# A fused strided-attention, MoE and FFN kernel: all strided heads in compact classes, another order of the first loads, up sums in place, three score buffers, a higher fill rate

## The chip, the cores and the metric

The kernel runs on one core of a Trainium2 chip. The metric is device time in microseconds of one execution. The core has a matmul engine (TensorE, PE in the profile), three engines for elementwise work (VectorE is DVE, ScalarE is ACT, GpSimd is POOL), SyncE (SP), which only issues DMA transfers here, and 16 DMA engines.

## The reference, cut to what matters

```python
# attention: q, k, v of 4 batches, 8 heads, 576 positions, 64 dimensions
scores = scale * np.matmul(q, k.transpose(0, 1, 3, 2))
rel = pos[:, None] - pos[None, :]
mask_local = (rel >= 0) & (rel < 32)
mask_strided = (rel >= 0) & (pos[None, :] % 32 == pos[:, None] % 32)
# heads 0..3 use mask_local, heads 4..7 mask_strided; softmax; times v
# MoE: 2304 tokens, 512 wide, 8 experts of 1024; gate weights balanced in 8 rounds
h = np.maximum(x @ w1[e], 0.0); out += P[:, e:e+1] * (h @ w2[e])
# FFN: 512 -> 2048 -> 512
h = x @ w_in; g = h / (1 + np.exp(-1.702 * h)); return g @ w_out
```

A strided head needs little of its 576 x 576 scores: position p sees only positions with the same remainder by 32, so the head falls into 32 classes of 18 positions each.

## The kernel before, in words

**Attention.** Heads are handled in pairs, pairs 0 and 1 local, 2 and 3 strided. The list `groups` (line 866 on) says in which order; an entry is (batch, pair, g). For g of 0 to 2 a group is *wide*: `att_scores` multiplies queries and keys of two pieces for two heads (for a strided pair a piece is seven classes of 18, 126 rows, and the third group has one piece of 72), VectorE masks and takes the maximum, ScalarE takes the exponential, GpSimd divides, `att_transpose` transposes on TensorE, `att_values` multiplies by the values. With g = -1 a group is *compact* and stands for a whole strided pair: `compact_scores` runs 64 small matmuls of 18 columns that place the classes side by side (each shows as two records in the trace), VectorE transposes 32 x 32 blocks, ScalarE copies the result into a zeroed wide tile (`ew`), and `compact_values` multiplies four classes at a time, 72 columns. Before the change batches 0 and 1 have their strided pairs compact, batches 2 and 3 wide, three groups each.

**Steps.** `att_step(i)` runs five stages for five neighbouring groups, so that a group's scores come at its step i, its values at i + 4. Between the stages `fill` puts other work on TensorE: idle matmuls for the first ten steps, a few half products and idle matmuls for the next six, and then *pieces*, RATE of them per fill, three fills a step. Queries and keys are loaded by `LOAD_QK`, values by `LOAD_V`, at the ends of steps worked out from `groups`.

**Pieces.** The MoE and the FFN are cut in units of 256 hidden columns for a block of 768 tokens. A unit is one round of a seven-product scheme: `PRODUCTS` lists seven products of an input (or a sum of inputs) with a weight quarter W or a sum of quarters T. Every operand is split in a high and a low part, and a product is six matmuls (`sum_of_six`, line 1017). A unit has 13 pieces: seven products (pieces 0, 2, ... 12 of the unit) and, between them, six times six matmuls with the down weights of the unit before (`tile_down`, lines 1282 to 1284). `side[g]` holds what is handed to the other engines after piece g.

**Weights.** For each of the 32 MoE units, the up weights are loaded (`load_w1`), GpSimd forms the four sums T1 to T4 (`sums_w1`, lines 235 to 237) in a tile of its own, and `split_w1` splits quarters and sums: ScalarE copies the high part (lines 258, 268), VectorE or GpSimd subtracts (line 252), and the result goes to the products and by DMA to a store in device memory for later blocks. `plan_weights` says at which piece each is handed out. The down weights get the same treatment (`plan_down_sums`, line 343).

**The start.** The loads stand in order: queries and keys of the first two pairs, one compact value, the first up weights, a second compact value, the first down weights, two compact values of batch 1, the gate weights, the second up weights; then come the attention's steps. Masks and constants go by ScalarE's queue. All on SP's queue is issued in order; a transfer into a buffer that is still read waits there.

Of the kernel before, what the change touches and what calls it, by code (L numbers as in the profile page):

```python
# [15 lines left out]
P = 128  # L16
# [20 lines left out]
RATE = 1.15  # L37
# [20 lines left out]
def strided_attention_moe_ffn(  # L58
# [26 lines left out]
    CPT = P // CLEN  # L85
# [142 lines left out]
    def sums_w1(i, t=None):  # L228

        r = raw[1, i]  # L230
        if t is None:
            t = rawp[0].tile([P, 4, 2 * P], F32, tag="sums", name="sums")
        g = nc.gpsimd
# [7 lines left out]
    WHERE = {"W11": (1, 0), "W12": (1, 1), "W21": (1, 2), "W22": (1, 3), "T1": (3, 0), "T3": (3, 1), "T2": (3, 2), "T4": (3, 3)}  # L241

    def quarter(i, what):
        which, q = WHERE[what]
        return raw[which, i][:, q, :]
# [84 lines left out]
    def plan_down_sums(dp, i, again=None):  # L330
# [59 lines left out]
    def plan_weights():  # L390

        for at, k in zip((10, 12, 14, 16, 18, 19, 21), range(NPR)):
            side[at].append(lambda k=k: split_w1(PLAIN, k))
        side[8].append(lambda: [t() for t in sums_w1(PLAIN)])
        for i in range(PLAIN - 1, NU):
            new = [fresh(u) for u in range(i, i + 3)]

            if PLAIN <= i < NU - 1:
                if new[1]:
                    side[piece_at(i, 0)].append(lambda i=i: [t() for t in sums_w1(i + 1)])  # L400
                for m, k in enumerate((0, 3, 5, 1, 2, 4, 6) if new[1] else range(NPR)):
                    at = max(m, 2 * (m - 2) + 1)
                    side[piece_at(i, at)].append(lambda i=i, k=k: split_w1(i + 1, k))
# [223 lines left out]
    wide_of = {}  # L627

    def open_wide(m):
        t = xcp.tile([P, 2 * CQ, CG * CLEN], F32, tag="xc", name="ew")  # L630
        nc.gpsimd.memset(t, 0.0)
        wide_of[m] = t
# [6 lines left out]
    def compact_scores(i, b, pair):  # L639
# [14 lines left out]
        e = ap.tile([P, 4 * P], F32, tag="e", name="e", bufs=4)  # L654
# [5 lines left out]
        def mask():  # L660
            for j in range(2):
# [4 lines left out]
                    in1=msk[:, None, 5 * P : 5 * P + CLEN].to_broadcast([P, CQ, CLEN]),  # L666
# [26 lines left out]
    def compact_transpose(i, b, pair):  # L693
# [3 lines left out]
        w = att[b, pair, -1] = wide_of[pair % 2]  # L697
        src = eT.rearrange("p n (m q) -> p (n m) q", q=Q)
        for c in range(CG):
            rows = slice(c * Q, c * Q + CLEN)  # L700
            nc.scalar.activation(out=w[rows, :, c * CLEN : (c + 1) * CLEN], in_=src[rows, :, :CLEN], func=AF.Copy)

    def compact_values(i, b, pair):
        w = att.pop((b, pair, -1))
# [3 lines left out]
        for h in range(2):  # L708
            if i < NALONE:
                av = ps.tile([P, 512], F32, tag="AB"[h], name="av")  # L710
            elif h:
                av = ps.tile([P, 512], F32, tag="B", name="av")
            else:
                av = eps.tile([P, 512], F32, tag="pa", name="av")
            for m in range(CQ // 2):
                g = h * CQ // 2 + m
                for j in range(2):
# [3 lines left out]
                        rhs=w[:, j * CQ + g, :],  # L721
# [14 lines left out]
    def geometry(pair, g, u):  # L736

        if pair < NPAIR // 2:
            q0 = (2 * g + u) * QT
            return q0, QT, max(0, q0 - STRIDE), P  # L740
        t = 2 * g + u
        c0 = t * CPT
        n = min(CPT, NCLS - c0) * CLEN
        return c0 * CLEN, n, c0 * CLEN, n

    def units(pair, g):
        return 2 if pair < NPAIR // 2 or g < 2 else 1

    def att_scores(i, b, pair, g):
        qkt = att_in["qk", b, pair]  # L750
        U = units(pair, g)

        sc = eps.tile([P, 2, 512], F32, tag="sc", name="sc")
        for u in range(U):
            for j in range(2):
                q0, R, k0, C = geometry(pair, g, u)
# [8 lines left out]
        e = ap.tile([P, 4 * P], F32, tag="e", name="e", bufs=4)  # L765
        st = ap.tile([P, 2, 4], F32, tag="st", name="st", bufs=4)
        m0 = 3 * P if pair >= NPAIR // 2 else P if g else 0
# [79 lines left out]
    def att_keep(b, pair, g, av, U, R):  # L847
        n = U * R
        if pair < NPAIR // 2:
            blk, at = divmod(b * S + g * 2 * QT, BT)  # L850
            nc.vector.tensor_copy(xblk[blk][:, pair, at : at + n], av[:, :n])
            return
        strided_keep(b, pair, 2 * g * CPT, n // CLEN, av)

# [16 lines left out]
    groups += [(b, pair, g) for b in range(2, B) for pair in PAIRS for g in range(3)]  # L871
# [13 lines left out]
    wide = [p for p in pairs if groups[at[p][0]][2] >= 0]  # L885
# [3 lines left out]
    for n, p in enumerate(wide):  # L889
        LOAD_V[max(at[wide[n - 2]][-1] + 4 if n > 1 else 0, at[p][0] + 1)].append(p)  # L890
# [530 lines left out]
    with tc.manual_schedule():  # L1421
# [209 lines left out]
```

## Time and profile before

| | before |
|---|---|
| runs, median (lowest to highest) | 1957.82 us (1957.12 to 1961.69) of 3 |
| profiled execution | 1956.79 us, its span 1955.0 us |
| TensorE busy, share of the span | 1919.4 us, 98% |
| VectorE, ScalarE, GpSimd busy | 1455.9, 864.3, 1242.0 us |
| mean granted TensorE clock | 0.994 of full |

The span is the part of the execution between the first and the last instruction. "Busy" is the time in which an engine has an instruction running. A row of the groups gives line, engine, operation, tiles, shapes and count, then busy time and mean time of one, then the idle time before it with what ended it. "<-DMA qkt<-qk" says that a wait ended when the transfer into `qkt` landed; "<-issue" that no semaphore or transfer that the profile knows ended it. Times of a timeline are us from the start of the span.

### The profile page before, as it was taken

How to read it: one execution, taken by the hardware profiler on the slowest of the kernel's cores; microseconds unless marked ns; L12 is line 12 of the kernel's file. 1: busy time of each engine (PE TensorE's matmuls, PEld its weight loads, DVE VectorE, ACT ScalarE, POOL GpSimd, SP SyncE). 2: the span in 40 equal slices, each digit the busy share in tenths (PEclk: the TensorE clock that was granted, in tenths of full speed). 3: DMA queues.
4: the chain of work that ended last, by engine and by line, in shares of the span. 5: the costliest groups of instructions: out<-in, count | busy, mean ns of one | idle time of the engine just before them, and what ended most of it. 6: DMA issues, size and time to landing. Idle time of an engine off the chain costs nothing.

```text
span 1955.0 us, 34399 instructions
## 1 busy us (share of the span) xinstructions
PE 1919.4 (98%) x11276; PEld 1793.0 (92%) x11276; DVE 1455.9 (74%) x2751; ACT 864.3 (44%) x2152; POOL 1242.0 (64%) x1249
## 2 busy tenths in 40 slices
PE   6999999999999999999999999999999999999999
PEld 5777888898888999999999999999999998888888
DVE  4787778777766788788878788888886766756555
ACT  4555556676665333333333433333333445533332
POOL 3456666777777677677777888888887767600100
PEclk8999999999999999999999999999999999999999
DMA  5457779999997898888898888999988867665653
GB/s 213 152 209 270 266 276 331 385 338 350 379 330 248 318 307 290 297 286 283 285 303 286 253 310 293 341 327 322 364 314 314 294 222 265 237 189 187 222 192 121
DMA packets 283649, 545.75 MB, mean 279 GB/s; under 512 B 30832, under 2 KB 51536, under 8 KB 282576
## 3 DMA queue, kind: packets, MB, share of 16 engines
q1 hardware_dynamic: 283184, 543.09, 80.5%
q8 instruction: 91, 1.49, 0.3%
q14 instruction: 86, 0.70, 0.1%
q10 hardware_dynamic: 288, 0.47, 0.1%
HBM read 381.90 MB, written 161.53 MB: 278 GB/s over the span
## 4 chain that ended last, share of the span: by engine, by line
PE 80%; DVE 2%; POOL 1%; ACT 0%; issue 0%; DMA 0%; ACTq 0%; DVEq 0%
PE y L1177 22%; PE pA L1017 22%; PE pC L1017 11%; PE y L1284 6%; PE y L1283 6%; PE y L1282 6%; PE pB L1017 5%; DVE xs L552 0%; POOL s L1149 0%; POOL comb L1124 0%; DVE comb L1124 0%; POOL xc L568 0%; DVE xc L572 0%; DVE r L1130 0%; DMA w<-s1moe 0%
## 5 line engine op out<-in xcount | busy, mean ns | idle before, releaser
L1017 PE MATMUL pA<-xc,w 128*128 128x384 f32 x2880 | 572.3, 336 | 1.9 <-DVE pB L1072 1.9
L1177 PE MATMUL y<-comb,w 128*128 128x384 f32 x2688 | 537.6, 334 | 1.4 <-DVE sum L1187 1.4
L1017 PEld LDWEIGHTS pA<-xc,w 128*128 128x128 f32 x2880 | 508.0, 188 | 18.8 <-DVE pB L1072 2.9
L1177 PEld LDWEIGHTS y<-comb,w 128*128 128x128 f32 x2688 | 472.0, 188 | 2.5 <-DVE sum L1187 2.4
L1124 POOL TENSOR_TENSOR comb<-s,comb 128x384 fp32r<-128x384 f32 x256 | 283.3, 1117 | 89.1 <-ACT comb L1119 82.4
L1187 DVE TENSOR_TENSOR sum<-y,sum 128x384 f32<-128x384 f32 x420 | 231.4, 552 | 98.5 <-PE y L1177 96.8
L1017 PE MATMUL pC<-xc,w 128*128 128x384 f32 x1464 | 295.0, 336 | 0.0
L1017 PEld LDWEIGHTS pC<-xc,w 128*128 128x128 f32 x1464 | 258.6, 188 | 10.0
L1284 PE MATMUL y<-w,hl 128*128 128x512 f32 x672 | 266.9, 397 | 0.4 <-DVE hl L1056 0.4
L1282 PE MATMUL y<-w,hh 128*128 128x512 f32 x672 | 263.4, 392 | 3.7 <-DVE acc L1297 2.0
L1283 PE MATMUL y<-w,hh 128*128 128x512 f32 x672 | 265.3, 395 | 0.0
L1119 ACT ACTIVATE comb<-r 128x384 fp32r<-128x384 f32 x192 | 101.0, 526 | 364.0 <-DVE r L1130 348.3
L252 POOL TENSOR_TENSOR w<-raw,w 128x512 fp32r<-128x512 f32 (+1 forms) x100 | 117.6, 1182 | 74.4 <-ACT w L258 69.9
L1284 PEld LDWEIGHTS y<-w,hl 128*128 128x128 f32 x672 | 125.9, 187 | 28.3 <-DVE hl L1056 1.0
L1282 PEld LDWEIGHTS y<-w,hh 128*128 128x128 f32 x672 | 126.2, 188 | 22.8 <-DVE acc L1297 2.6
L1017 PE MATMUL pB<-xc,w 128*128 128x384 f32 x708 | 142.4, 335 | 0.0
L1283 PEld LDWEIGHTS y<-w,hh 128*128 128x128 f32 x672 | 126.0, 187 | 15.9
L1124 POOL TENSOR_TENSOR comb<-r,comb 128x384 fp32r<-128x384 f32 x64 | 67.5, 1054 | 114.4 <-ACT comb L1119 114.4
L1119 ACT ACTIVATE comb<-s 128x384 fp32r<-128x384 f32 x256 | 131.5, 514 | 11.0 <-POOL s L1149 10.9
L1149 POOL TENSOR_TENSOR s<-r,r 128x384 f32<-128x384 f32 x127 | 134.8, 1082 | 2.1 <-DVE r L1130 2.0
L1311 DVE TENSOR_TENSOR acc<-y,acc 128x512 f32<-128x512 f32 x126 | 86.8, 689 | 63.3 <-PE y L1284 63.1
L1017 PEld LDWEIGHTS pB<-xc,w 128*128 128x128 f32 x708 | 125.2, 188 | 4.7
(178 smaller groups left out, 2878.0 us busy)
## 6 DMA issues: line engine op xcount, KB each, us to landing
w<-s1moe SPq DMA_DIRECT2D x448, 256.0 KB, 4.9
w<-s7moe SPq DMA_DIRECT2D x448, 256.0 KB, 4.9
s1moe<-w SPq DMA_DIRECT2D x216, 256.0 KB, 4.5
w<-s1ffn SPq DMA_DIRECT2D x133, 256.0 KB, 2.7
s7moe<-kw SPq DMA_DIRECT2D x116, 256.0 KB, 4.9
s7moe<-w SPq DMA_DIRECT2D x96, 256.0 KB, 4.7
w<-s2ffn SPq DMA_DIRECT2D x38, 512.0 KB, 3.7
raw<-wa SPq DMA_DIRECT2D x32, 512.0 KB, 5.9
```

The lines of the kernel that those rows point to most:

```text
L252: eng.tensor_tensor(out=t[:, 1], in0=src, in1=f(high), op=ALU.subtract)
L1017: nc.tensor.matmul(out=o, lhsT=w[:, hw, kk * P : (kk + 1) * P], rhs=x[:, hx, kk, :], start=opens and m == 0, stop=ends and m == len(todo) - 1,
L1119: nc.scalar.activation(out=t[:, 0, :], in_=part[i, q], func=AF.Copy)
L1124: eng.tensor_tensor(out=t[:, 1, :], in0=part[i, q], in1=f(t[:, 0, :]), op=ALU.subtract)
L1149: eng.tensor_tensor(out=part[i, q], in0=part[i, a], in1=part[i, b], op=op)
L1177: nc.tensor.matmul(out=o, lhsT=t[:, hw, dt * P : (dt + 1) * P], rhs=x[:, hx, :], start=(n == 0), stop=(n == 5))
L1187: nc.vector.tensor_tensor(out=a, in0=o, in1=a, op=ALU.add)
L1282: nc.tensor.matmul(out=o, lhsT=hh[:, c], rhs=w[:, 0], start=(m == 0), stop=False)
L1283: nc.tensor.matmul(out=o, lhsT=hh[:, c], rhs=w[:, 1], start=False, stop=False)
L1284: nc.tensor.matmul(out=o, lhsT=hl[:, c], rhs=w[:, 0], start=False, stop=(m == 1))
L1311: nc.vector.tensor_tensor(out=a, in0=y, in1=a, op=ALU.add)
```

## The change

All strided pairs become compact: batches 2 and 3 now have four compact groups in place of twelve wide ones, so the list of groups shrinks from 40 to 32 and the steps from 44 to 36. `RATE` goes from 1.15 to 1.5. One zeroed tile `wide` takes the place of two; the score tiles `e` have three buffers in place of four; the values' buffer is eight pieces long in place of six. The first loads are put in another order: queries and keys, then two compact values, and the weights and the values of batch 1 after the first attention steps. For MoE units `sums_w1` writes T1 to T4 over the quarters they no longer need, after the quarters' own splits, with another order and other pieces in `plan_weights` and `plan_down_sums`.

```diff
-RATE = 1.15
+RATE = 1.5
@@ sums_w1
+        if t is None and UNITS[i][1] == "moe":
+            steps = [(0, 1, 0), (1, 3, 1), (3, 3, 0), (2, 2, 3)]
+            todo = [
+                lambda o=o, a=a, b=b: g.tensor_tensor(
+                    out=r[:, o, :], in0=r[:, a, :], in1=r[:, b, :], op=ALU.subtract
+                )
+                for o, a, b in steps
+            ]
+            return todo + [lambda: placed.add(i)]
@@ plan_down_sums
-            at = piece_at(i, ((3, 3, 4, 5), (0, 1, 1, 2))[i == S0 - 1][m]) if again is None else piece_at(again, 5 + m)
+            at = piece_at(i, ((1, 1, 2, 2), (0, 1, 1, 2))[i == S0 - 1][m]) if again is None else piece_at(again, 5 + m)
@@ plan_weights
-        for at, k in zip((10, 12, 14, 16, 18, 19, 21), range(NPR)):
+        for at, k in zip((10, 12, 14, 16, 18, 19, 21), (0, 3, 5, 1, 2, 4, 6)):
-        side[8].append(lambda: [t() for t in sums_w1(PLAIN)])
+        side[15].append(lambda: [t() for t in sums_w1(PLAIN)])
+                moe = UNITS[i + 1][1] == "moe"
-                    side[piece_at(i, 0)].append(lambda i=i: [t() for t in sums_w1(i + 1)])
+                    side[piece_at(i, 4 if moe else 0)].append(lambda i=i: [t() for t in sums_w1(i + 1)])
-                    at = max(m, 2 * (m - 2) + 1)
+                    at = (0, 1, 2, 5, 7, 8, 9)[m] if new[1] and moe else max(m, 2 * (m - 2) + 1)
@@ load_v
-        t = ap.tile([P, 6, P], F32, tag="v", name="vt")
-        nc.sync.dma_start(out=t, in_=vw[b, pair])
+        t = ap.tile([P, CQ, P], F32, tag="v", name="vt")
+        compact = pair >= NPAIR // 2
+        src = vc[b, pair - NPAIR // 2] if compact else vw[b, pair]
+        nc.sync.dma_start(out=t if compact else t[:, : vw.shape[3]], in_=src)
+    wide = ap.tile([P, 2 * CQ, CG * CLEN], F32, name="wide", bufs=1)
@@ compact_scores, att_scores
-        e = ap.tile([P, 4 * P], F32, tag="e", name="e", bufs=4)
+        e = ap.tile([P, 4 * P], F32, tag="e", name="e", bufs=3)
@@ compact_transpose (compact_values reads wide too)
-        w = att[b, pair, -1] = wide_of[pair % 2]
-            nc.scalar.activation(out=w[rows, :, c * CLEN : (c + 1) * CLEN], in_=src[rows, :, :CLEN], func=AF.Copy)
+            nc.scalar.activation(out=wide[rows, :, c * CLEN : (c + 1) * CLEN], in_=src[rows, :, :CLEN], func=AF.Copy)
@@ groups
-    groups += [(b, pair, g) for b in range(2, B) for pair in PAIRS for g in range(3)]
+    for b in range(2, B):
+        groups += [(b, pair, -1) for pair in PAIRS[:2]]
+        groups += [(b, pair, g) for pair in PAIRS[2:] for g in range(3)]
@@ loads
-    wide = [p for p in pairs if groups[at[p][0]][2] >= 0]
+    ring = [p for p in pairs if p[0] > 1 or p[1] < NPAIR // 2]
-    for n, p in enumerate(wide):
-        LOAD_V[max(at[wide[n - 2]][-1] + 4 if n > 1 else 0, at[p][0] + 1)].append(p)
+    for n, p in enumerate(ring):
+        LOAD_V[max(at[ring[n - 2]][-1] + 4, at[p][0] + 1) if n > 1 else n + 2].append(p)
@@ the start
-        load_vc(0, PAIRS[0])
         nc.scalar.dma_start(out=cst, in_=consts)
-        load_w1(0)
-        load_vc(0, PAIRS[1])
-        load_w2(0)
-        for m in range(2):
-            open_wide(m)
         for pair in PAIRS[:2]:
-            load_vc(1, pair)
+            load_vc(0, pair)
+        nc.gpsimd.memset(wide, 0.0)
@@ ahead: what is handed out after a step
-        load_w1(1)
+        ahead[1].append(lambda: load_w1(0))
+        ahead[3].append(lambda: load_w2(0))
+        ahead[4].append(lambda: load_w1(1))
+        for m, pair in enumerate(PAIRS[:2]):
+            ahead[5 + m].append(lambda pair=pair: load_vc(1, pair))
         for n, what in enumerate(QUARTERS):
-            ahead[3 + 2 * n].append(lambda what=what: split_plain(0, what))
+            ahead[(4, 5, 7, 8)[n]].append(lambda what=what: split_plain(0, what))
```

## Rows read from the trace of the kernel before

**Rows 1.** The page's busy line: us, share of the span, instructions.

```profile
PE 1919.4 (98%) x11276; PEld 1793.0 (92%) x11276; DVE 1455.9 (74%) x2751; ACT 864.3 (44%) x2152; POOL 1242.0 (64%) x1249
```

**Rows 2.** Busy time by stage: columns PE, PEld, DVE, ACT, POOL; clock, DMA, GB/s.

```profile
10.00:20.00 10.00, 2.60 (x52) 2.08 (x52) 2.22 (x7) 1.24 (x3) 0.67 (x1) 0.60 1.00 380
...
95.00:237.00 142.00, 137.55 (x932) 111.72 (x930) 110.79 (x251) 83.43 (x299) 87.10 (x94) 1.00 0.70 248
```

**Rows 3.** The same view, a stretch of the dense part.

```profile
500.00:600.00 100.00, 100.00 (x501) 89.98 (x500) 68.23 (x134) 67.62 (x185) 78.17 (x90) 1.00 0.95 340
```

**Rows 4.** Timeline 0 to 40: start, us, engine, line, operation, tiles, [idle before].

```profile
6.09 1.27 PE L646 MATMUL sc<-qkt 64*32 64x18 f32 x128 [1.52 <-DMA qkt<-qk]
...
8.18 0.88 PE L646 MATMUL sc<-qkt 64*32 64x18 f32 x82
...
9.51 4.80 SPq L619 DMA_DIRECT2D qkt<-qk  x2
...
13.26 0.70 PE L646 MATMUL sc<-qkt 64*32 64x18 f32 x46 [4.19 <-issue]
...
20.00 1.17 PE L757 MATMUL sc<-qkt 64*96 64x128 f32 x8 [4.14 <-DMA qkt<-qk]
...
26.02 2.19 PE L718 MATMUL av<-ew,vc 128*64 128x72 f32 x32 [1.24 <-ACT ew L701]
...
31.26 1.22 PE L718 MATMUL av<-ew,vc 128*64 128x72 f32 x32 [0.89 <-issue]
```

**Rows 5.** Busy time in stretches of 5 us at the start, columns as in group 2.

```profile
5.00:10.00 5.00, 2.97 (x214) 2.60 (x214) 1.44 (x4) 0.93 (x1) 0.00 (x0) 1.00 1.03 412
...
15.00:20.00 5.00, 0.86 (x4) 0.38 (x3) 1.32 (x5) 0.44 (x1) 0.67 (x1) 0.50 0.95 372
20.00:25.00 5.00, 4.78 (x22) 3.28 (x22) 3.66 (x8) 0.91 (x3) 0.67 (x1) 0.50 0.04 18
```

**Rows 6.** Timeline 40 to 72, TensorE.

```profile
51.24 0.90 PE L838 MATMUL av<-eT,vt 128*64 128x96 f32 x6 [2.46 <-issue]
...
54.49 2.11 PE L1017 MATMUL pA<-xc,w 128*128 128x384 f32 x6
```

**Rows 7.** The loads of queries and keys (tile qkt), SP.

```profile
DMA to landing us min/median/max: 3.6/5.3/10.3
```

**Rows 8.** Groups by shape, TensorE, 0 to 620: busy us, mean ns, idle before.

```profile
L718 PE MATMUL av<-ew,vc 128*64 128x72 f32 x128 | 5.9, 254 | 2.1 <-ACT ew L701 1.2 <-issue 0.9
L757 PE MATMUL sc<-qkt 64*126 64x126 f32 x64 | 5.7, 294 | 2.2 <-DMA qkt<-qk 2.2
L646 PE MATMUL sc<-qkt 64*32 64x18 f32 x512 | 5.6, 192 | 6.2 <-issue 4.7 <-DMA qkt<-qk 1.5
L838 PE MATMUL av<-eT,vt 126*64 126x126 f32 x64 | 5.2, 284 | 0.0
L814 PE MATMUL pt<-cst,e 126*126 126x126 f32 x32 | 5.2, 284 | 0.1
...
L757 PE MATMUL sc<-qkt 64*72 64x72 f32 x16 | 1.4, 252 | 0.0
L838 PE MATMUL av<-eT,vt 72*64 72x72 f32 x16 | 1.4, 252 | 0.0
L814 PE MATMUL pt<-cst,e 72*72 72x72 f32 x8 | 1.3, 241 | 0.0
```

**Rows 9.** Timeline 158 to 172, TensorE.

```profile
169.76 0.71 PE L757 MATMUL sc<-qkt 64*126 64x126 f32 x8 [2.24 <-DMA qkt<-qk]
```

**Rows 10.** Timeline 388 to 424, SP's queue.

```profile
402.27 0.33 SPq L225 DMA_DIRECT2D raw<-wb  x1
```

**Rows 11.** Timeline 400 to 418, GpSimd.

```profile
407.40 1.75 POOL L235 TENSOR_TENSOR sums<-raw 128x512 f32<-128x512 f32 x1
...
411.44 1.45 POOL L343 TENSOR_TENSOR dsums<-raw 128x256 f32<-128x256 f32 x2
```

**Rows 12.** The loads of raw weights (tile raw), 320 to 620, SP.

```profile
DMA to landing us min/median/max: 4.2/6.0/9.0
```

More of the change, by code (lines that the diff above doesn't have):

```diff
@@ L241, in strided_attention_moe_ffn @@
     WHERE = {"W11": (1, 0), "W12": (1, 1), "W21": (1, 2), "W22": (1, 3), "T1": (3, 0), "T3": (3, 1), "T2": (3, 2), "T4": (3, 3)}
+    placed = set()
     def quarter(i, what):
         which, q = WHERE[what]
+        if which == 3 and i in placed:
+            which, q = 1, (0, 1, 3, 2)[q]
         return raw[which, i][:, q, :]
@@ L710, in compact_values @@
                 av = ps.tile([P, 512], F32, tag="AB"[h], name="av")
+            elif i >= NFIRST:
+                av = down_bank("av")
             elif h:
@@ L720, in compact_values @@
                         lhsT=vt[:, g, j * HD : (j + 1) * HD],
-                        rhs=w[:, j * CQ + g, :],
+                        rhs=wide[:, j * CQ + g, :],
                         start=True,
@@ L734, in strided_attention_moe_ffn, with geometry @@
     }
[L736 to L747, printed above, removed]
+    def geometry(g, u):
+        q0 = (2 * g + u) * QT
+        return q0, QT, max(0, q0 - STRIDE), P
     def att_scores(i, b, pair, g):
         qkt = att_in["qk", b, pair]
-        U = units(pair, g)
+        U = 2
         sc = eps.tile([P, 2, 512], F32, tag="sc", name="sc")
@@ L755, in att_scores @@
             for j in range(2):
-                q0, R, k0, C = geometry(pair, g, u)
+                q0, R, k0, C = geometry(g, u)
                 nc.tensor.matmul(
@@ L764, in att_scores @@
         n = 2 * U
-        e = ap.tile([P, 4 * P], F32, tag="e", name="e", bufs=4)
+        e = ap.tile([P, 4 * P], F32, tag="e", name="e", bufs=3)
         st = ap.tile([P, 2, 4], F32, tag="st", name="st", bufs=4)
-        m0 = 3 * P if pair >= NPAIR // 2 else P if g else 0
+        m0 = P if g else 0
         s = e[:R, : n * C].rearrange("p (n c) -> p n c", n=n)
@@ L848, in att_keep @@
         n = U * R
[L849 to L853, printed above, removed]
+        blk, at = divmod(b * S + g * 2 * QT, BT)
+        nc.vector.tensor_copy(xblk[blk][:, pair, at : at + n], av[:, :n])
     def strided_keep(b, pair, c0, n, av):
@@ L1556 @@
     NP, CL = H // 2, S // STRIDE
-    CPT = P // CL
     def columns(x):
@@ L1567 @@
     qk = np.ascontiguousarray(np.stack([columns(q), columns(k)], axis=3))
-    vw = np.zeros((B, NP, P, 6, 2, HD), v.dtype)
+    vw = np.zeros((B, NP // 2, P, 6, 2, HD), v.dtype)
     vp = v.reshape(B, NP, 2, S, HD)
-    vs = vp.reshape(B, NP, 2, CL, STRIDE, HD).transpose(0, 1, 2, 4, 3, 5).reshape(B, NP, 2, S, HD)
     for u in range(6):
         k0 = max(0, u * QT - STRIDE)
-        vw[:, : NP // 2, :, u] = vp[:, : NP // 2, :, k0 : k0 + P].transpose(0, 1, 3, 2, 4)
-        if u < 5:
-            a, z = u * CPT * CL, min((u + 1) * CPT * CL, S)
-            vw[:, NP // 2 :, : z - a, u] = vs[:, NP // 2 :, :, a:z].transpose(0, 1, 3, 2, 4)
-    vw = vw.reshape(B, NP, P, 6, P)
-    vc = np.zeros((2, NP // 2, 4, 32, 8, 2, HD), v.dtype)
-    vc[:, :, :, :CL] = (
-        vs[:2, NP // 2 :].reshape(2, NP // 2, 2, 8, 4, CL, HD).transpose(0, 1, 4, 5, 3, 2, 6)
-    )
-    vc = vc.reshape(2, NP // 2, P, 8, P)
+        vw[:, :, :, u] = vp[:, : NP // 2, :, k0 : k0 + P].transpose(0, 1, 3, 2, 4)
+    vw = vw.reshape(B, NP // 2, P, 6, P)
+    vs = vp[:, NP // 2 :].reshape(B, NP // 2, 2, CL, 8, 4, HD)
+    vc = np.zeros((B, NP // 2, 4, 32, 8, 2, HD), v.dtype)
+    vc[:, :, :, :CL] = vs.transpose(0, 1, 5, 3, 4, 2, 6)
+    vc = vc.reshape(B, NP // 2, P, 8, P)
     def up_tiles(w):
@@ L1605 @@
     neg = np.float32(MASKED)
-    masks = np.zeros((P, 5 * P + CL), np.float32)
-    masks[:, 5 * P :][(i % 32)[:, None] < np.arange(CL)[None, :]] = neg
+    masks = np.zeros((P, 3 * P + CL), np.float32)
+    masks[:, 3 * P :][(i % 32)[:, None] < np.arange(CL)[None, :]] = neg
     for n, rel in enumerate((first, later, later)):
         masks[:, n * P : (n + 1) * P][(rel < 0) | (rel >= STRIDE)] = neg
-    rows = CPT * CL
-    for n in range(2):
-        part = masks[:, 3 * P + n * rows : 3 * P + (n + 1) * rows]
-        part[((first < 0) | (i[:, None] // CL != i[None, :] // CL))[:, :rows]] = neg
     consts = np.zeros((P, 2 * P), np.float32)
```

11 lines of the change are left out of this document (2 added, 9 removed).

## The prediction

> **What bounds the kernel now.** I read the page's busy line first, then the busy time by stage, then the start in order of time, then the attention's instructions with shapes kept apart.
>
> The busy line [rows 1] says that TensorE is the bound: 1919.4 of 1955.0 us. The stages say where part of the other 36 us lies [rows 2]: in 10:20 TensorE works 2.60 of 10 us, in 95:237 it lacks 4.45 of 142 us. A stretch of the dense part is full [rows 3]. So there are three ways to a shorter time: begin the dense part earlier, take matmul work out, take gaps out of the attention. In the dense part a faster engine or an earlier load is worth nothing, as long as no new wait appears.
>
> The start [rows 4]: the scores of the first compact group run at 6.09, of the second at 8.18, those of the third step only at 20.00, after a wait that ends with its queries and keys. In 15:20 the DMA engines are 0.95 busy at 372 GB/s, in 20:25 they are nearly idle [rows 5]. Those queries and keys were issued at 9.51, behind three weight loads and four compact values, so the third step waits for bytes that nothing needs yet. One more thing is late: the second group stops after 82 of its 128 score matmuls and goes on 4.19 us later with "issue" as the reason, that is, no semaphore and no transfer of data [rows 4]. The first product of the weights starts at 54.49 [rows 6], in the eleventh attention step, and from there on the kernel is nearly dense. What the third step gains, the first product gains, if the steps between keep their lengths.
>
> **The change, part by part.**
>
> *Queue order.* Ahead of the third step's queries and keys stand now (sizes from the tiles' shapes) two queries and keys of 0.59 MB, the masks, the constants and two compact values of 0.52 MB: 2.6 MB, where three weight pieces and two more values, another 2.6 MB, stood too. At the 372 to 412 GB/s of [rows 5] those first 2.6 MB take 7 us, so they are in by 9 or 10. The third queries and keys still reuse the first one's buffer, so they are issued when the first scores end, at about 7.4; a landing of 3.6 to 5.3 us [rows 7] puts them at 11 to 13. But TensorE works in order and must finish the second group's scores first: with the same "issue" gap these end at 13.96, with a shorter one at 12 or so. So the third step starts at 12.5 to 14 instead of 20.00, a gain of 6 to 7.5. The fourth step's queries and keys go out when the second scores are done and land at 17 to 19; the values of the fifth step, which came 6.02 us after the third step's scores (26.02 less 20.00, [rows 4]), would stand at 18.5 to 20. So this load is just hidden, and if it takes the longest landing of the trace (10.3) it costs 3 to 4. The moved weight loads go out in steps 1 to 6, into a stretch where the DMA engines now do nearly nothing (0.04 busy in 20:25, [rows 5]), and are wanted from step 4 on; behind them in SP's queue stand only later loads and stores. I take -6.5, bounds -2.5 and -9 (the second if the half clock is left sooner: the grant in 10:20 averages 0.60, [rows 2]).
>
> *Compact classes for batches 2 and 3.* Out go twelve wide groups (eight of 126 rows, four of 72). Their matmuls are the rows of 126 and 72 [rows 8]: 5.7 + 1.4 for scores, 5.2 + 1.3 for transposes, 5.2 + 1.4 for values, 20.2 us. In come four compact groups. The four of the trace took 5.6 us of scores and 5.9 of values [rows 8], so 11.5 again; their transposes run on VectorE. That is -8.7. Bounds: with values at 2.19 us a group, the cluster at half clock [rows 4], and scores at 1.27, it is -6.4; at the fastest clusters, 1.27 + 1.22 us [rows 4], it is -10.2.
> The price of 18-column matmuls is the term that a rule speaks against. The trace has 128 of them in 1.27 us, some 10 ns each [rows 4]. The Trainium skill (TensorE: Matmul & The Clock Gate, section "Wait — 56ns, not 53.3ns?") says that two matmuls never start less than about 25 ns apart, however few their columns. By that a group's 128 take 3.2 us and this part gives only -1.5, an estimate from that page; the row contradicts it at the very shape, and I go by the row.
>
> *Fewer steps at a higher rate.* The attention has 44 steps before and 36 after; 28 full-rate steps of 3 x 1.15 pieces become 20 of 3 x 1.5. The pieces done inside it are 10 + 97 before and 10 + 90 after, and the loop that closes the stage runs on to piece 106, where it was 107. So the same work lies ahead of the gate steps, and only gaps can change. 95:237 lacks 4.45 us in some 27 steps; eight fewer make it -1.3, bounds 0 and -3.
>
> *Up sums in place.* GpSimd runs four subtractions of 256 columns in place of one of 512 and two of 256: the same columns. They move from piece 0 to piece 4, behind the down sums, and the splits of the sums move from pieces 3 to 9 into 5 to 9. The products that read them come from piece 15 on, ten pieces later, so TensorE sees nothing directly: 0. Two covers are thin. The down sums, now first, need a load issued at 402.27 [rows 10] for a unit whose up sums began at 407.40 [rows 11]; with a landing of 6.0 us [rows 12] it is there at 408.3, where the down sums of before began at 411.44. And ScalarE copies the first sum one piece after GpSimd is handed it, where it had three. If GpSimd is late by a piece or more, ScalarE stands in its queue, with the copies and activations of the products behind it.
>
> *One buffer for the transposed weights, three for the scores.* The copies of a second compact group now wait for the values of the first; both come in the same step in that order already. The fourth score buffer was free a step earlier; now the clearing of a buffer on GpSimd waits for the transposes of the same step, and what is queued behind are splits with pieces of slack. 0, bounds 0 and +2 over the four new groups.
>
> *Loads inside the shorter attention.* The values of four pairs, and the queries and keys of four, now go out one step before they are needed. One such load is late in the trace, by 2.24 us [rows 9]. The steps get longer, since each holds 4.5 pieces for 3.45. So 0, bounds 0 and +8 (all eight late by half of that, or four by all of it).
>
> Sum: -6.5 - 8.7 - 1.3 = -16.5 against the profiled execution's 1956.8 us (1955.0 of it span), 1940.3. That execution is 1.0 under the median of the runs shown, so I say 1940.5.
>
> **The rivals.**
>
> *The start gains little* (0.10). For it: the 4.19 us "issue" gap, and the fourth step's load that is only just hidden. Against: the third step waited for data by name. With -2.5 at the start the time is 1944.3, with nothing 1946.8.
>
> *New short stalls in the attention eat the second gain* (0.13). Compact groups use up instructions fast: 128 weight loads and 128 matmuls in 1.27 us. After the two of batch 1 TensorE stood 2.46 us in the middle of a values cluster, with "issue" as the reason [rows 6]. Two more such pairs cost 4.9, the late loads up to 8. With both at half to full size the time is 1947 to 1953. Against: between two new compact groups lie 4.5 pieces of slow matmuls, where those two had three fills of idle matmuls between them. The Trainium skill (Runtime: NRT & Kernel Launch, "Instruction fetch mechanics") says that fetching the next block of instructions is mostly hidden; by that the "issue" part of this rival would be 0, which the 2.46 us does not bear out.
>
> *The small matmuls don't stream among products* (0.02). If one of 18 columns cost what one of 72 does (32 in 1.22 us, [rows 4], 38 ns), 128 would take 4.9 us, four groups 25.4 instead of 11.5, and the time would be 1954. Against: the 1.27 us. By the rule of the clock-gate page of the Trainium skill it would be 1947.5.
>
> *The sums in place stop the dense part* (0.09). The place: each of the 29 moe units with fresh weights after the plain ones. ScalarE waits for a sum that GpSimd is handed at piece 4, and the bank copies behind it hold TensorE. At 0.6 us a unit (17 us) the whole gain is gone, at 1 us the time is 1969: slower. Against: in 500:600 GpSimd is busy 78 of 100 us and ScalarE 68 [rows 3], so each has room, and TensorE shows no gap there.
>
> **How the numbers follow.** The forecast (start, matmuls and steps as summed) has 0.66; its own range is 1934 to 1946. The range goes up through the first two rivals to 1951. Down, all three terms at their far bounds (-9 - 10.2 - 3) give 1934.6, and without the two gaps of 2.24 and 2.46 us it is 1930. What a measurement of this kernel can tell from no change is about 0.3%, 6 us: faster means under 1952. Faster: 0.66 + 0.10 + half of the second rival, 0.83; same: its other half, the third rival and a small fourth, 0.10; slower: the rest of the fourth, 0.07.
>
> **What would show it.** The scores of the third step at 12.5 to 14 us, the first product near 48 instead of 54.49. The rows of 126 and 72 gone, 1024 records of 18 columns in about 11 us. The last attention values near 212 instead of 237 (the gains, and seven pieces fewer inside). After that the same dense units as in [rows 3], shifted. Wrong: a dense part with ScalarE waiting for GpSimd's sums and TensorE below 100 of 100 us; "issue" or load gaps over 2 us in the new compact steps; a first product still after 52.

## The result: slower

After: median 1972.02 us (1968.06 to 1978.84, 6 runs); before, on the same chip: 1957.52 us (1956.76 to 1962.17, 6 runs). The ratio is 1.0069, interval 1.0048 to 1.0090, so the change costs 0.7%. I had forecast 1940.5, in 1930 to 1951. The profiled execution of after took 1968.06 us with a span of 1966.3, 11.3 us more than before. It is the fastest of the six, so what its trace shows accounts for 11.3 of the 14.5 us between the medians; the slowest of the six, 1978.84 us, has a mean granted clock of 0.985 where this one has 0.991. In the kernel after, the lines have moved by 1 to 10: compact scores L656, compact values L728, wide scores L759, products L1018, down products L1283 to L1285.

The busy line of after, against [rows 1]:

```profile
PE 1918.5 (98%) x11716; PEld 1794.6 (91%) x11716; DVE 1451.3 (74%) x2723; ACT 856.8 (44%) x2087; POOL 1241.2 (63%) x1274
```

TensorE is busy as long as before, in a longer span: 47.8 us idle where it was 35.6. The stages of after (columns as in [rows 2]) say where:

```profile
10.00:20.00 10.00, 6.15 (x88) 4.80 (x89) 6.32 (x15) 3.01 (x9) 1.35 (x2) 0.83 0.73 256
...
95.00:150.00 55.00, 49.76 (x604) 41.39 (x605) 41.38 (x88) 30.54 (x98) 25.71 (x29) 0.94 0.58 198
150.00:200.00 50.00, 43.63 (x332) 36.80 (x321) 36.03 (x79) 26.51 (x83) 28.66 (x34) 0.97 0.74 267
200.00:237.00 37.00, 33.80 (x203) 27.97 (x203) 24.46 (x49) 17.19 (x52) 21.03 (x26) 1.00 0.70 247
237.00:330.00 93.00, 85.20 (x460) 73.09 (x459) 70.63 (x172) 46.76 (x128) 58.78 (x75) 0.96 0.80 280
330.00:500.00 170.00, 168.88 (x839) 150.59 (x838) 126.23 (x241) 113.77 (x315) 124.14 (x152) 1.00 0.97 352
500.00:600.00 100.00, 100.00 (x500) 89.75 (x499) 68.81 (x137) 68.31 (x188) 77.39 (x95) 1.00 0.96 343
```

In 10:20 the earlier start shows: 6.15 us of work for 2.60 [rows 2]. Between 95 and 237 TensorE now lacks 14.8 of 142 us (it lacked 4.45), and the granted clock is 0.94 and 0.97 in the first two of these stretches, where it was 1.00. From 330 on little is missing, and 500:600 is as full as in [rows 3].

The start of after, TensorE in order of time, against [rows 4] and [rows 6]:

```profile
11.11 0.69 PE L656 MATMUL sc<-qkt 64*32 64x18 f32 x46 [2.60 <-issue]
13.63 1.04 PE L759 MATMUL sc<-qkt 64*96 64x128 f32 x8
...
45.13 0.80 PE L840 MATMUL av<-eT,vt 128*64 128x96 f32 x6 [2.47 <-issue]
...
48.27 2.12 PE L1018 MATMUL pA<-xc,w 128*128 128x384 f32 x6
```

The third step's scores come at 13.63 instead of 20.00, the first product at 48.27 instead of 54.49: -6.2, where the sum had -6.5. The shapes of after, 0 to 620, against [rows 8]:

```profile
L656 PE MATMUL sc<-qkt 64*32 64x18 f32 x1024 | 10.6, 190 | 3.9 <-issue 2.8 <-DMA qkt<-qk 1.1
L728 PE MATMUL av<-wide,vt 128*64 128x72 f32 x128 | 6.1, 244 | 8.0 <-DVE acc L1298 6.0 <-DMA vt<-vc 2.0
```

The rows of 126 and 72 are gone, and the 1024 small records took 10.6 us, some 10 ns each. (By the rule that the prediction weighed from the Trainium skill, TensorE: Matmul & The Clock Gate, section "Wait — 56ns, not 53.3ns?", 25 ns from start to start, an estimate for the 1024 records is 25.6 us, and for the kernel's 512 matmuls, each of which shows as two records, 12.8; the trace agrees with neither.) The second row has the news: 8.0 us of waits ahead of the new groups' values.

The waits by kind (us in all, times, longest), TensorE, 55 to 260, first of after and then of before:

```profile
PE av L728 <- DVE acc L1298: 6.0, 2, 3.6
PE sc L759 <- DMA qkt<-qk: 2.8, 2, 2.0
PE y L1283 <- DVE x L852: 2.0, 2, 1.5
PE av L728 <- DMA vt<-vc: 2.0, 1, 2.0
PE pt L816 <- DVE x L861: 1.9, 1, 1.9
PE y L1283 <- ACT hh L1054: 1.7, 1, 1.7
```

```profile
PE sc L757 <- DMA qkt<-qk: 2.2, 1, 2.2
PE pt L814 <- DVE x L862: 1.8, 1, 1.8
PE y L1282 <- DVE acc L1297: 1.5, 2, 1.0
PE sc L757 <- DVE e L772: 0.6, 1, 0.6
```

**How far behind.** Both kernels run the same 5052 product matmuls in the same order, so the start of the n-th in each gives the lag of one against the other. By the times of before: -6.2 us at the first product (54.5), +3.2 at 290, when both have their attention behind them, +8.8 at 345, +10.8 at 427, +11.3 at 1940. So 9.4 us are lost in the attention though 8.7 us of matmuls went out of it, and its last values start at 229.4 (237.3 before), where the prediction had them near 212. Another 7.6 are lost between 290 and 427, 5.6 of them by 345, in the stretch of the gate's steps (where the gate weights are balanced), and 0.5 in the 1500 us after.

From the first product to number 822 (427 us) I split the time, from matmul records and granted clock, into TensorE's idle time, half of its busy time at a granted half clock (what the full clock would have saved), and the rest, the work: before 10.1, 1.0 and 360.2 us; after 26.6, 10.0 and 351.7. The work fell by 8.5, as forecast; idle rose by 16.5 and the half-clock loss by 9.0. Together +17.0, less 6.2 at the start: +10.8.

One place shows how such a loss is built. After, 98 to 116, ScalarE first, then VectorE, then TensorE:

```profile
101.33 0.85 ACT L576 ACTIVATE xc<-S 128x768 fp32r<-128x768 f32 x1 [3.95 <-DVE S L565]
105.02 1.85 ACT L710 ACTIVATE wide<-eT 18x288 f32<-18x288 f32 x4 [2.83 <-DVE eT L706]
106.89 0.49 ACT L1054 ACTIVATE hh<-pC 128x384 fp32r<-128x384 f32 x1
...
109.69 0.83 ACT L576 ACTIVATE xc<-S 128x768 fp32r<-128x768 f32 x1
```

```profile
110.55 0.96 DVE L581 TENSOR_TENSOR xc<-S,xc 128x768 fp32r<-128x768 f32 x1 [1.71 <-ACT xc L576]
...
112.02 0.68 DVE L1298 TENSOR_TENSOR acc<-y,acc 128x512 f32<-128x512 f32 x1
```

```profile
102.11 0.68 PE L759 MATMUL sc<-qkt 64*96 64x128 f32 x8
...
107.43 0.51 PE L1283 MATMUL y<-w,hh 128*128 128x512 f32 x1 [1.67 <-ACT hh L1054]
...
108.46 0.72 PE L728 MATMUL av<-wide,vt 128*64 128x72 f32 x16
112.75 1.23 PE L728 MATMUL av<-wide,vt 128*64 128x72 f32 x16 [3.57 <-DVE acc L1298]
113.91 1.17 PE L759 MATMUL sc<-qkt 64*96 64x128 f32 x8
```

ScalarE waits for VectorE's transposes, makes the four copies, and only then the activation `hh` that TensorE wants. The next input's copy comes at 109.69, VectorE waits for it with the sum of a down product behind it, and that sum frees the bank that the second half of the compact values needs. TensorE stands 3.57 us and then runs slower: 1.23 us for 16 matmuls that had just taken 0.72, 1.17 for scores that took 0.68.

### The profile page after: what moved, and what is told of

Read it like the earlier page. It is cut to its first block, busy times and chain, and to the rows that moved or that the text cites. A ratio compares the mean times of both kernels' runs of the same rounds, so it can differ in the third digit from the quotient of the medians.

```text
span 1966.3 us, 35166 instructions
## 1 busy us (share of the span) xinstructions
PE 1918.5 (98%) x11716; PEld 1794.6 (91%) x11716; DVE 1451.3 (74%) x2723; ACT 856.8 (44%) x2087; POOL 1241.2 (63%) x1274
## 4 chain that ended last, share of the span: by engine, by line
PE 76%; DVE 2%; DMA 1%; POOL 1%; issue 1%; ACT 0%; SPq 0%; ACTq 0%; DVEq 0%
PE y L1178 22%; PE pA L1018 21%; PE pC L1018 10%; PE y L1285 6%; PE y L1284 6%; PE y L1283 6%; PE pB L1018 5%; DMA acc<-kept 0%; POOL s L1150 0%; DVE xs L565 0%; POOL comb L1125 0%; DMA w<-s7moe 0%; DMA s7moe<-w 0%; DVE r L1131 0%; DVE comb L1125 0%
## 5 line engine op out<-in xcount | busy, mean ns | idle before, releaser
L1018 PE MATMUL pA<-xc,w 128*128 128x384 f32 x2880 | 572.4, 336 | 1.8 <-DVE pB L1073 1.8
L1018 PEld LDWEIGHTS pA<-xc,w 128*128 128x128 f32 x2880 | 508.3, 188 | 18.2 <-DVE pB L1073 2.8
L1018 PE MATMUL pC<-xc,w 128*128 128x384 f32 x1464 | 296.4, 337 | 0.0
L1285 PE MATMUL y<-w,hl 128*128 128x512 f32 x672 | 268.5, 400 | 4.9 <-DVE hl L1057 4.7
L1018 PEld LDWEIGHTS pC<-xc,w 128*128 128x128 f32 x1464 | 260.4, 189 | 10.0 <-issue 0.3
L1283 PE MATMUL y<-w,hh 128*128 128x512 f32 x672 | 264.6, 394 | 4.9 <-DVE x L852 2.0
L1285 PEld LDWEIGHTS y<-w,hl 128*128 128x128 f32 x672 | 126.7, 189 | 35.0 <-DVE hl L1057 7.6
L1283 PEld LDWEIGHTS y<-w,hh 128*128 128x128 f32 x672 | 127.0, 189 | 24.8 <-DVE x L852 3.0
L1018 PE MATMUL pB<-xc,w 128*128 128x384 f32 x708 | 142.1, 335 | 0.0
L270 ACT ACTIVATE w<-raw 128x256 fp32r<-128x256 f32 (+1 forms) x307 | 135.9, 461 | 10.4 <-POOL raw L234 10.3
```

Source lines behind the costliest of these rows:

```text
L270: nc.scalar.activation(out=high, in_=src, func=AF.Copy)
L1018: nc.tensor.matmul(out=o, lhsT=w[:, hw, kk * P : (kk + 1) * P], rhs=x[:, hx, kk, :], start=opens and m == 0, stop=ends and m == len(todo) - 1,
L1283: nc.tensor.matmul(out=o, lhsT=hh[:, c], rhs=w[:, 0], start=(m == 0), stop=False)
L1285: nc.tensor.matmul(out=o, lhsT=hl[:, c], rhs=w[:, 0], start=False, stop=(m == 1))
```

## The experiments

A lag is always that of the products against the profiled execution of before. My first theory was the row with the longest wait: the values of the new compact groups need two banks of the down products' ring (the banks that the down products use in turn) one after the other, and the ring is the bound. Its rivals were the higher rate, the sums in place with the new pieces of their splits (the fourth rival of the prediction, at another place), and late loads. A ratio is that of a run to the kernel before on the same chip, with its 95% interval. Letters in the expectations are names of theories: those up to F stand for these first causes, G for three splits in a row that hold ScalarE and the activations behind them, H for the four copies of a compact group that do so.

**e1_pa**, after with the first half of the compact values in a bank of its own:

```diff
-            elif i >= NFIRST:
+            elif i >= NFIRST and h:
                 av = down_bank("av")
```

> The changed kernel, but the first half of the late compact values goes into the attention's own bank (pa) instead of a second bank of the down products' ring. Theory A (two ring banks in a row are what TensorE waits for: the two waits on the accumulation, 3.6 and 2.4 us, and the half clock after them): those two waits go, the time falls by 6 to 12 us, to 1960 to 1966. Rival B (the rate of 1.5 overloads the stages around it) and rival C (the sums in place): the waits move to other instructions, the time stays within 3 us of 1972.

1970.28 us, ratio 1.0055 (1.0040 to 1.0070). TensorE's waits, 55 to 250:

```profile
PE av L728 <- DMA vt<-vc: 5.1, 1, 5.1
PE pt L816 <- DVE x L861: 4.6, 2, 2.7
```

The wait of 6.0 us for the ring is gone; the two lines that stand there now make 9.7 us, where after had 3.9. The lag at 290 is 1.4 (3.2 in after), and at 427 11.0 (10.8): the ring by itself is not the cause.

**e2_rate**, after at the old rate:

```diff
-RATE = 1.5
+RATE = 1.15
```

> The changed kernel with RATE back at 1.15. Rival B (4.5 pieces a step put too much in front of the attention's own copies and additions): the gaps in the attention go down to the 4 or 5 us of before and the time falls by 10 to 20 us, to 1952 to 1962. Theory A: the values still need two ring banks in a row, and the loads that go out one step ahead now have shorter steps, so the gaps stay and the time is within 4 us of 1972, if anything higher.

1971.74 us, 1.0064 (1.0042 to 1.0086): the old rate by itself gives nothing back. It doesn't clear the rate of all blame, since it brings what theory A had foreseen: with the shorter steps one load of a compact group's values kept TensorE waiting for 7.3 us.

**e3_start**, before with the new order of the first loads alone:

```diff
-        load_vc(0, PAIRS[0])
...
-        load_w1(0)
-        load_vc(0, PAIRS[1])
-        load_w2(0)
+        for pair in PAIRS[:2]:
+            load_vc(0, pair)
...
+        ahead[1].append(lambda: load_w1(0))
+        ahead[3].append(lambda: load_w2(0))
+        ahead[4].append(lambda: load_w1(1))
```

> The kernel before with the new order of the first loads alone. If the start's gain of 6.2 us at the first product is handed on, the time is 1951 to 1952 (ratio 0.997). Rival: an earlier start only makes the steps behind it wait (for weights that now come later), and the time is 1956 to 1958.

1955.13 us, 0.9975 (0.9964 to 0.9986): the gain is real, and not all of it reaches the end. The lag is -5.3 at the first product, -5.1 at 150 and -2.0 at 201. Between the last two lie these lines of TensorE:

```profile
160.55 0.39 PE L1282 MATMUL y<-w,hh 128*128 128x512 f32 x1
164.95 1.22 PE L757 MATMUL sc<-qkt 64*126 64x126 f32 x8 [2.49 <-DMA qkt<-qk]
168.18 0.63 PE L1282 MATMUL y<-w,hh 128*128 128x512 f32 x1
```

A wait of 2.49 us for a load (2.24 before, [rows 9]), and behind it 0.63 us for a matmul that takes 0.39. Up to product 822 the loss by half clock is 6.1 us here, where before has 1.0.

**e4_sums**, before with the sums in place and their new pieces alone (the parts of the diff in `sums_w1`, `quarter`, `plan_down_sums` and `plan_weights`):

```diff
-                    at = max(m, 2 * (m - 2) + 1)
+                    at = (0, 1, 2, 5, 7, 8, 9)[m] if new[1] and moe else max(m, 2 * (m - 2) + 1)
```

> The kernel before with the up sums in place and their new pieces alone. Rival C (the sums in place hold ScalarE and VectorE, and with them TensorE): 1963 to 1972, with gaps before the down products in 290 to 440 us. Theory A: 1957 to 1960, at most the 2 us that the changed kernel loses between 345 and 437 us.

1971.74 us, 1.0059 (1.0041 to 1.0076): this part, priced at 0, costs nearly as much as the whole change. The lag is 1.0 at 201, 8.7 at 237, 8.1 at 290, 11.8 at 345 and 13.2 at 427: the larger part is lost in the attention, and not behind 290, where the expectation had it. Its longest wait, TensorE, and the issue of that load on SP's queue (200 to 212):

```profile
210.53 1.17 PE L771 MATMUL sc<-qkt 64*96 64x128 f32 x8 [4.20 <-DMA qkt<-qk]
```

```profile
200.41 0.89 SPq L269 DMA_DIRECT2D s7moe<-dsums  x1
201.40 0.57 SPq L269 DMA_DIRECT2D s1moe<-w  x1
202.39 0.32 SPq L269 DMA_DIRECT2D s7moe<-kw  x1
202.81 0.52 SPq L633 DMA_DIRECT2D qkt<-qk  x1
```

The load of queries and keys goes out behind stores of split weights, and TensorE starts 7.7 us after its issue, late by 4.20.

**e6_sched**, before with only the pieces of e4_sums, the sums in a tile of their own. 

> The kernel before, its sums in a tile of their own, but with the changed pieces: up sums at piece 4, down sums first, splits of sums at pieces 5 to 9. Theory D (the sums handed out later bunch up on GpSimd, their stores come later in SP's queue, and the loads of queries and keys behind them land late): 1966 to 1972, as with the sums in place, with waits for qkt over 5 us in all. Rival E (writing over the quarters, so that GpSimd waits for the splits, is what costs): 1957 to 1961.

1970.85 us, 1.0053 (1.0038 to 1.0069). So it is the pieces, not the overwriting. The way that theory D gives isn't shown: the waits for qkt are 3.7 us in all (55 to 260), not over 5, and 7.5 in e4_sums.

**e7_actq**, after with the attention's loads on ScalarE's queue:

```diff
-        nc.sync.dma_start(out=t, in_=qk[b, pair])
+        nc.scalar.dma_start(out=t, in_=qk[b, pair])
...
-        nc.sync.dma_start(out=t if compact else t[:, : vw.shape[3]], in_=src)
+        nc.scalar.dma_start(out=t if compact else t[:, : vw.shape[3]], in_=src)
```

> The changed kernel with the loads of queries, keys and values of the attention issued by ScalarE's queue, out of the way of the stores. Theory D: the waits of TensorE for qkt and vt (2.8 and 2.0 us after 54) go, with the half clock that follows them, 1963 to 1968. Rival F (what costs in the changed kernel are the compact groups' waits on the accumulation and on VectorE): those stay, 1970 to 1975, and ScalarE loses some us to the issues.

1974.15 us, 1.0070 (1.0053 to 1.0087). No wait for a load is left among the longer ones of 55 to 345, but values wait 8.2 us for the ring and a gate transpose 3.9 for VectorE. In this kernel late loads by themselves are not the cause.

**e8_start_actq**, e3_start with the loads on ScalarE's queue. 

> The kernel before with the new order of the first loads and with the attention's loads on ScalarE's queue. Theory D: the 2.5 us wait for qkt and the 6.8 us of half clock behind it go: 1949 to 1952. Rival: the issues on ScalarE delay the exponentials and the time stays at 1954 to 1957.

1956.89 us, 0.9984 (0.9975 to 0.9993), no better than e3_start.

**e9_start_sums**, the load order of e3_start and the sums of e4_sums, no new compact groups. 

> The kernel before with the new order of the first loads and the sums in place, without the compact groups of batches 2 and 3 and at the old rate. If the parts add up, -4 + 12.6: 1965 to 1969; then the compact groups and the rate, which take out 8.7 us of matmuls, cost 3 to 7 us more than they save. If they do save what was forecast, this stands 8 to 10 above the changed kernel: 1978 to 1982.

1963.23 us, 1.0019 (1.0007 to 1.0031): 0.44% above e3_start, 8.6 us for the sums. The kernel after lies another 0.50%, 9.8 us, above this one: the new compact groups, with their rate, buffers and loads, cost that, where the sum had -10.0. (The profiled execution of e9_start_sums, 1959.93 us, is one of its fastest.)

**e10_spaced**, after with the last splits spaced out:

```diff
-                    at = (0, 1, 2, 5, 7, 8, 9)[m] if new[1] and moe else max(m, 2 * (m - 2) + 1)
+                    at = (0, 1, 2, 5, 7, 9, 11)[m] if new[1] and moe else max(m, 2 * (m - 2) + 1)
```

> The changed kernel with the splits of the four sums at pieces 5, 7, 9, 11 in place of 5, 7, 8, 9. Theory G (three splits in a row fill the two halves of ScalarE's staging bank, ScalarE waits for VectorE, and the activations behind it come late: the loss of 6 to 8 us between 285 and 345 us): that loss falls to 2 or 3, 1965 to 1969. Rival (what costs is that the sums themselves are later): no change, 1970 to 1974.

1963.76 us, 1.0025 (1.0014 to 1.0036). Two numbers give back 0.44%, 8.6 us. In the gate's steps, 250 to 330, TensorE's longest wait of after is the first line, the same one of e10_spaced (250 to 345) the second:

```profile
PE y L1285 <- DVE hl L1057: 3.6, 2, 3.2
```

```profile
PE y L1285 <- DVE hl L1057: 2.1, 1, 2.1
```

The lag is -1.7 at 290 (3.2 in after), 1.5 at 427 (10.8), but 4.7 at 600 (10.9). These 3.2 us in the dense part are not the price of the later splits alone: with the same splits e13_nocompact_spaced loses 1.4 there and e15_spaced_pa_actq 0.2. That the pieces of the last two splits cost much of the time is shown; that it is because three came in a row, and not because of the pieces they fell on, is the nearest reading, but one that no run tells apart. The way that the expectation gives, ScalarE waiting for the two halves of its staging bank, is not: that wait is 10.2 us in after between 237 and 345, and 16.6 in before. What the lines of after show at that wait of 3.2 us is VectorE, which has the splits' low parts, the gate's small steps and `hl` in one queue:

```profile
298.94 0.41 DVE L264 TENSOR_TENSOR w<-raw,high 128x256 fp32r<-128x256 f32 x1
...
300.56 0.41 DVE L972 TENSOR_REDUCE sk<-pr 128x8 f32<-128x144 f32 x1
300.89 0.41 DVE L264 TENSOR_TENSOR w<-raw,high 128x256 fp32r<-128x256 f32 x1
301.22 0.68 DVE L1298 TENSOR_TENSOR acc<-y,acc 128x512 f32<-128x512 f32 x1
301.82 0.55 DVE L1057 SCALAR_TENSOR_TENSOR hl<-pC,hh 128x384 fp32r<-128x384 f32 x1
```

```profile
302.42 0.79 PE L1285 MATMUL y<-w,hl 128*128 128x512 f32 x1 [3.21 <-DVE hl L1057]
```

**e11_copies**, after with the four copies of a compact group handed to ScalarE behind the exponentials of the same step:

```diff
-        for c in range(CG):
-            rows = slice(c * Q, c * Q + CLEN)
-            nc.scalar.activation(out=wide[rows, :, c * CLEN : (c + 1) * CLEN], in_=src[rows, :, :CLEN], func=AF.Copy)
+        def copies():
+            for c in range(CG):
...
+        return (copies,)
```

> The changed kernel with ScalarE's four copies into the wide tile handed out after the step's exponentials and first fill, not at the start of the step. Theory H (ScalarE stands 2 to 3 us for VectorE's transposes and 1.85 us in the copies, with the activations that TensorE needs behind them): idle TensorE and half clock before 250 us fall by 4 to 10 us, 1962 to 1968. Rival (the values' two ring banks, or the loads, are what holds TensorE whatever ScalarE does): no change, 1970 to 1974, or later values and worse.

1980.78 us, 1.0119 (1.0100 to 1.0139): the values then wait 10.9 us for the copies themselves. **e12_both**, the same with the spaced splits. 

> Both edits of the two runs before it. If G and H are separate causes the gains add up: 1956 to 1964. If only one of them is one, it is that run's time.

 1970.67 us, 1.0063 (1.0047 to 1.0080). The copies ahead of `hh` are the lesser evil: theory H's gain doesn't come. Moving the copies only trades one wait for another, so what the copies' own time costs is not shown.

**e13_nocompact_spaced**, e9_start_sums with the spaced splits. 

> The kernel before with the new order of the first loads, the sums in place, and the splits of the sums at pieces 5, 7, 9, 11. Theory G: most of what the new pieces cost goes, 1955 to 1959, against 1963 with 5, 7, 8, 9. Rival (the later sums cost): 1961 to 1965.

1958.69 us, 1.0001 (0.9990 to 1.0012): 5 us under e10_spaced in the same comparison. The two differ by the compact groups of batches 2 and 3 with their rate, buffers and loads. Taken together these take some 9 us of work out and make the kernel slower. Idle and half-clock loss to product 822 are 13.0 and 3.2 here, 21.0 and 6.6 in e10_spaced.

**e14_spaced_pa**, e10_spaced with the bank of e1_pa. 

> The changed kernel with the splits at 5, 7, 9, 11 and the first half of the late compact values in the attention's own bank. Theory A' (the wait for the second ring bank, 2 to 3 us twice, and the 10 us of half clock behind the first one are what the compact groups cost): 1952 to 1958. Rival L (another late thing takes its place: the values' load, which had 5.1 us in the run with the bank alone, or the transposes that share the bank): 1959 to 1964.

 1961.93 us, 1.0019 (1.0004 to 1.0033); the values wait 4.9 us for their load, transposes 4.7 for VectorE.

**e15_spaced_pa_actq**, this with the loads on ScalarE's queue. 

> The same with the attention's loads on ScalarE's queue. If the loads are the other half of it (rival L): 1948 to 1955 and no wait for vt or qkt after 60 us. If ScalarE is what is late, its queue gets longer by the issues and the time stays at 1957 to 1963.

 1961.04 us, 1.0013 (1.0002 to 1.0023). With ring and loads out of the way one kind of wait over 2 us is left, TensorE, 55 to 250:

```profile
PE pt L816 <- DVE x L861: 8.3, 3, 3.6
```

That is the bank of e1_pa, which the transposes of the wide groups share, until VectorE has taken the compact values out of it (1.9 us of such waits stood in after too). The interval of this run overlaps with that of e13_nocompact_spaced: with both edits the compact groups are no longer shown to be slower than none, nor are they faster.

**e16_rate125**, e15_spaced_pa_actq with

```diff
-RATE = 1.5
+RATE = 1.25
```

> The same with RATE 1.25 in place of 1.5. Rival B (the rate puts too many copies and additions between the attention's own): 3 to 6 us below the run before it. If the rate only moves work from behind the attention into it, within 3 us of it.

 1969.11 us, 1.0051 (1.0031 to 1.0071): worse; the same wait is 7.2 us, and a 4.1 us "issue" gap stands at compact scores.

**e17_first_pa_actq**, e15_spaced_pa_actq with that bank only for the first of two compact groups:

```diff
-            elif i >= NFIRST and h:
+            elif i >= NFIRST and (h or groups[i + 1][2] >= 0):
```

> Splits at 5, 7, 9, 11, loads on ScalarE's queue, and the attention's own bank only for the first compact group of a batch, in whose step no transposes run on TensorE. If the bank's two waits are the rest of the cost: the 2.9 and 3.9 us of the transposes and the half clock after them go, 1950 to 1955, under the kernel before and under the run without compact groups (1958.7). If VectorE is late whatever waits for it: another wait of 2 to 4 us in the same steps, 1957 to 1962.

 1962.11 us, 1.0015 (1.0005 to 1.0025). **e18_first_pa**, the same with the loads on SP. 

> The same with the loads on SP's queue. If the loads stand late there (4.9 us for vt in the run with the bank): 3 to 7 us above the run before it. If not, within 2 us of it.

 1962.39 us, 1.0019 (1.0010 to 1.0028). In both the waits are split over ring, bank, `hl` and, in the second, the values' load (4.1 us).

| lag of the products, us, at (times of before) | 54.5 | 150 | 290 | 427 | 600 | 1940 |
|---|---|---|---|---|---|---|
| after | -6.2 | 1.6 | 3.2 | 10.8 | 10.9 | 11.3 |
| e3_start | -5.3 | -5.1 | -1.1 | -1.6 | -1.3 | -1.3 |
| e4_sums | -0.1 | 2.1 | 8.1 | 13.2 | 13.4 | 14.2 |
| e9_start_sums | -6.6 | -4.5 | -3.2 | 1.8 | 1.9 | 3.0 |
| e13_nocompact_spaced | -4.9 | -3.6 | -0.8 | 0.3 | 1.7 | 2.1 |
| e10_spaced | -6.1 | -0.4 | -1.7 | 1.5 | 4.7 | 6.2 |
| e15_spaced_pa_actq | -5.3 | 0.1 | -1.4 | 1.5 | 1.7 | 3.2 |

The columns 54.5, 290 and after compare like with like; at 150 the kernels with compact groups have done another share of their attention. These are single executions. From 290 to 427, the gate's steps and what follows them, the three rows with splits at pieces 7, 8, 9 lose 7.6, 5.1 and 5.0 us, the three with 7, 9, 11 lose 1.1, 3.2 and 2.9, and e3_start, with the old pieces, gains 0.5. There the new pieces cost in all of these kernels. What they cost before 290 depends on the rest: 8.2 us in e4_sums, but in e9_start_sums no more than e3_start loses there (3.4 and 4.2).

The compact groups without the sums in place were not tried. Every version with the new compact groups also has the one tile `wide` and the three score buffers, so what these cost was not measured by itself. In after ScalarE waits once for `wide`, 3.3 us, until TensorE has read the values of the group before; in e15_spaced_pa_actq that wait is not there, and the time is still no better than before.

## Why the prediction was wrong

*Queue order, -6.5:* right. The third step's scores are at 13.63 (12.5 to 14 forecast), the first product gains 6.2. By itself this part brings 0.25%, 4.9 us, at the end (e3_start).

*Compact matmuls, -8.7:* right as work. The work to product 822 falls by 8.5. But none of it reaches the time, see the steps below.

*Up sums in place, 0: failed, by 8.6 us.* The prediction named two thin covers, and both tore. GpSimd's down sums now wait for the raw load (0.8 us before), and ScalarE's splits for GpSimd's sums (no such wait before). After, 237 to 440:

```profile
POOL dsums L355 <- DMA raw<-wb: 20.0, 9, 3.4
```

```profile
ACT w L270 <- POOL raw L234: 2.9, 2, 1.8
```

But I looked for the harm in the 29 dense units, and in 500:600 TensorE stays at 100.00 of 100 us. It lay where the fourth rival did not look: in the attention and in the gate's steps, where VectorE and ScalarE have other work in the same queues. I checked ten pieces of slack for the products that read the sums, and not what three splits in pieces 7, 8, 9 do to the activations queued behind them. By e9_start_sums against e3_start that costs 8.6 us, by e4_sums and e6_sched alone 10 to 12; other pieces for two of the splits give back 8.6 in after, and 3.5 in e9_start_sums (e13_nocompact_spaced). So the fourth rival came true in kind (slower, by the sums), with a chance of 0.09, at another place.

*Fewer steps, -1.3, and buffers and loads, 0: wrong in sign, and the largest miss.* With the compact matmuls these terms came to -10.0; on top of start and sums (after against e9_start_sums) they cost 9.8 us, so nearly 20 of the 31.5 us by which the result lies over the forecast are missed here. The step that failed is that gaps go with the number of steps: that with eight steps fewer, each fuller, those that remain keep their waits. Between these two kernels, up to product 822, the work falls by 9.5 us, TensorE's idle time rises by 11.3 and the loss by half clock by 6.8. The loads' upper bound of 8 held: after waits 2.8 and 2.0 us for queries and values. But when one wait was freed (the ring's, the loads', the copies' order: e1_pa, e7_actq, e11_copies, e14 to e18), another took its time. The second rival (0.13) had the direction and half of the size: its 1953 is 12.5 us over the forecast, and the range, 1930 to 1951, did not even take in that end of it. I compared each engine's load as an average: between 95 and 237 VectorE has 110.79 of 142 us [rows 2], which seemed room enough for 4.5 pieces a step in place of 3.45. The lines of 98 to 116 point to the order within one step instead; no run isolates it.

*Half clock: not priced.* The loss by it went from 1.0 to 10.0 us. Several of the gaps shown above (2.47, 3.57 and 3.21 us in after) have a slow stretch behind them as well.

What stays open: what makes the steps with compact groups late once the splits are spaced. The rate, the ring, the loads and the place of the copies were each varied, and none alone gives back the 5 us between e10_spaced and e13_nocompact_spaced (bank and loads together, e15_spaced_pa_actq, lie 0.12% under e10_spaced, with intervals that overlap). No version with the new compact groups came under before. The fastest of all, by its ratio, is e3_start, the first load order alone: 1955.13 us, 0.9975.

## What to carry to other kernels

Price a moved operation by what is queued behind it on each in-order engine at the busiest step, not by its slack to its reader nor by the engine's busy share. Work taken off the bounding engine pays only if its waits don't grow by as much: here 8.5 us of matmuls went out, and more than that came back as idle and half-clock time. Where a gap is freed and the time stays, look at the lag of a common series of instructions rather than at single waits.

## What the runs showed of the hardware that was not expected

**A short gap can cost more than itself, and need not.** In e3_start a gap of 2.49 us is followed by matmuls of 512 columns at 0.63 us, where the last before it took 0.39; in e4_sums one of 4.20 by scores at 1.17 us, where the same row at 199.81 took 0.68. In after the granted clock of 95:150 is 0.94 and of 237:330 0.96; before, 95:237 was at 1.00 [rows 2]. But before, the matmuls behind the gap of 2.24 us took 0.71 us [rows 9], the time at full clock, and so did those behind a gap of 2.88 us in e10_spaced:

```profile
171.82 0.72 PE L728 MATMUL av<-wide,vt 128*64 128x72 f32 x16 [2.88 <-DVE acc L1298]
172.47 0.68 PE L759 MATMUL sc<-qkt 64*96 64x128 f32 x8
```

The length of a gap alone doesn't tell; what else decides, no run here shows.

**The "issue" gaps of compact groups are not regular.** After has 2.60 us at the second group (4.19 before, [rows 4]), 2.38 ahead of the first compact values (none before, where ScalarE's copies ended the wait) and 2.47 in a values cluster, and none of 1 us at the four new groups; at other rates one of 2.8 (e2_rate) and one of 4.1 (e16_rate125) came back. The Trainium skill (Runtime: NRT & Kernel Launch, "Instruction fetch mechanics") calls the fetching of instructions mostly hidden; these gaps don't bear that out, if that is what they are, which no run here shows.
